# Attention reads, a Fourier mix and an MLP on one core: the first axis of batch 0 copied ahead of the last table sines and the Exp table load

## The chip, the core and the metric

The kernel runs on one core of a Trainium2 chip. The metric is the device time of one execution, in microseconds, as the median of several executions. Inside a profile, times count from the first instruction of the span (325.0 us in the profiled execution).

A core has TensorE (PE: matmuls, and PEld: its weight loads), VectorE (DVE), ScalarE (ACT), GpSimd (POOL) and SyncE (SP, which here only issues transfers). Each engine works through its own instructions in the order of the program and waits where a buffer or an operand is not ready. All engines are scheduled by hand in this kernel: the order of the calls in the source is the order on each engine.

## The reference, cut to what matters

`x` is 8 x 8 x 512 x 64 (batch, head, position, depth), `state` is 8 x 8 x 32 x 64. Positions read from the state, the state reads from the positions, and both go together into a Fourier mix over 544 positions and 512 channels, followed by a normalised two-layer MLP.

```python
def _attn_ref(x, state):
    scores = scale * np.matmul(x, state.transpose(0, 1, 3, 2))
    ...                                     # softmax over the 32 state rows
    xread = np.matmul(a, state)
    scores2 = scale * np.matmul(state, x.transpose(0, 1, 3, 2))
    ...                                     # softmax over the 512 positions
    sread = np.matmul(a2, x)
    return np.concatenate([xread, sread], axis=2)

def _moe_ref(x, w_ch1, w_ch2):              # x: 8 x 544 x 512
    X = np.fft.fft(x, axis=1)
    X = np.fft.fft(X, axis=2)
    u = x + np.real(X)
    ...                                     # mean and variance over the channels
    un = (u - mu) / np.sqrt(var + 1e-06)
    ch = np.maximum(un @ w_ch1, 0.0) @ w_ch2
    return u + ch
```

The real part of the two transforms is computed as matmuls with tables of cosines and sines: first over the positions ("the first axis", tables CT, ST and, for the rows from 256 on, CL and SL), then over the channels (tables TE and TO). The symmetry of the tables is used: inputs are folded first (XE, XO, XQ), so that fewer rows have to be multiplied.

## The kernel before

Batches are worked through as a pipeline. For each batch, `attend` gives the reads, `transform` the Fourier mix U, its mean and its centred and transposed copy, `layer1` and `layer2` the MLP. The opening is special, because the tables have to be made and nothing of a batch before is there to fill TensorE. `warm(n)` are n matmuls of 128 columns whose result nobody reads; they keep TensorE busy in the opening.

The tables, all on ScalarE (the arguments q1, f1, q2_, f2 come from DVE):

```python
    def sines():
        w = 2.0 * PI / Stot * shrink
        nc.scalar.activation(CT, q1[:, 0:2, :], AF.Sin, bias=halfpi, scale=-w)
        nc.scalar.activation(ST, f1[:, 0:2, :], AF.Sin, bias=0.0, scale=w)
        nc.scalar.activation(CL[0:32, 0, :], q1[0:32, 2, :], AF.Sin, bias=halfpi[0:32], scale=-w)
        nc.scalar.activation(SL[0:32, 0, :], f1[0:32, 2, :], AF.Sin, bias=0.0, scale=w)

    def more_sines():
        # ... eight sines of 128 columns: TE and TO (L241 to L248) ...
        w = 2.0 * PI / Stot * shrink
        nc.scalar.activation(cl1, q1[:, 2, :], AF.Sin, bias=halfpi, scale=-w)      # L250
        nc.scalar.activation(sl1, f1[:, 2, :], AF.Sin, bias=0.0, scale=w)          # L251
        nc.scalar.activation(gate2[:, 3:4], gate2[:, 0:1], AF.Exp)                 # L252
```

`cl1` and `sl1` are the low tables: GpSimd copies them into CL and SL for batches 1 to 3 (and 5 to 7). The Exp at the end, of one column, is there to have ScalarE's table for Exp loaded before the scores of batch 1 need it; Sin and Exp have different tables.

`more_loads` holds what GpSimd does next, in order: two sign rows of TO, the cast of x of batch 1 (behind a small copy that waits for the last XQ of batch 0), some clears, the low tables' copies, the load of x of batch 2, the casts of the state, and the load of w2 (behind a small copy that waits for x of batch 2).

x of a batch is transposed on TensorE and copied out of PSUM (batch 0 to 2):

```python
        def turn_x(g):
            # ... b >= 3: by transfers ...
            p = psF.tile([128, 1024], BF16, name="xTp", tag="c") if b == 1 else qt("xTp", BF16)
            for si in (0, 1, 3, 2):
                for k in range(2):
                    o = k * 512 + si * 128
                    nc.tensor.transpose(p[:, o:o + 128], xin[:, si, ...], ident)
            (nc.vector.tensor_copy if b == 0 or g == (b == 1) else nc.scalar.copy)(
                xT[:, 2 * g:2 * g + 2, :], p.rearrange("p (a b) -> p a b", b=S))        # L346
```

`qt` takes a buffer of a PSUM pool with three of them. The first axis, four products `gp`, each copied to one part of G; XQ[:, j] are the folded inputs, made by DVE one after the other:

```python
        def over_s(j):
            p = qt("gp")
            tab = cos if j < 2 else sin
            for c in range(3):
                nc.tensor.matmul(p[:, 0:NM], lhsT=XQ[:, j, c, :], rhs=tab[c], ...)     # L505
            if j == 2:
                for c in range(3):
                    nc.tensor.matmul(p[:, 0:NM], lhsT=XN[:, c, :], rhs=cos[c], ...)    # L509
            if b == 0 and j == 3:
                nc.vector.tensor_copy(G[:, j, :], p[:, 0:NM])                          # L511
            else:
                nc.scalar.copy(G[:, j, :], p[:, 0:NM])                                 # L513
            ...
```

The second axis (`second_axis`, L470 and L471) multiplies all four parts of G with TE and TO into `yp`, in the order of parts 0, 2, 1, 3; U is `yp` plus the read (L475, DVE), then come mean and variance (L302, L304, DVE), the centred copy `ub` (L537, ScalarE, for batches 0 and 1), its transposes on TensorE (L548) and their copy `unT` (L549), which layer 1 reads (L635 for batch 0).

The order of the opening. `t0` are the steps of `transform(0)`: 0 to 3 the four products of the first axis, 4 and 8 the second axis of the two row tiles, 5, 6, 10, 11 U and ub, 7, 9, 12, 13 the transposes of ub. `s1` are batch 1's steps up to its scores (0 its state's transposes, 1 and 2 those of x, 3 to 6 scores), `r1` its reads (0 and 1 the first two, 3 to 5 and 7 the others and the fold), `L` and `M` the two layers of batch 0:

```python
    weave((warmed(r0, 4), 0, 1), ([sines], 0.25, 0.25), ([more_sines], 0.3, 0.3), ([lambda: warm(44)], 1, 1))
    more_loads()
    load_x(3)
    ...
    for step in (warmed(t0[:4], 2) + [
            t0[4], t0[8], W(6), s1[1], W(4), t0[5], s1[0], W(16), t0[7], t0[6], s1[2], L[0], s1[3], t0[9], L[1], t0[10], s1[4],
            L[2], t0[11], t0[12], L[3], s1[5], L[4], s1[6], t0[13], r1[0], L[5], L[6], r1[1],
            L[7], r1[3], L[8], r1[4], L[9], r1[5], L[10], r1[7], late_cast]):
        step()
```

`late_cast` has GpSimd cast x of batch 2. After this list come the rest of layer 1, layer 2 and the pipeline of batches 1 to 7.

Of the kernel before, what the change touches and what calls it, by code (L numbers as in the profile page):

```python
# [28 lines left out]
def kernel(  # L29
# [8 lines left out]
    nc = tc.nc  # L38
# [72 lines left out]
    def load_x(b):  # L111
        xs = wk.tile([128, 4, dm], F32, name="xs", tag="xs")
        xb = x[b].rearrange("h s d -> s h d")
        for n, (ps, si, rows) in enumerate((
            (slice(0, 128), 2, xb[256:384]),
            (slice(0, 128), 0, xb[1:129]),
            (slice(0, 128), 1, xb[129:257]),
            (slice(0, 128), 3, xb[384:512]),
            (slice(0, 1), 2, xb[0:1]),
        )):  # L120
            queue = nc.scalar if b == 0 and n in (1, 3) else nc.sync
            queue.dma_start(out=xs[ps, si, :].rearrange("p (h d) -> p h d", d=D), in_=rows)
        xs_of[b] = xs

    def cast_x(b):
        xs, t = xs_of[b], xin_bufs[b % 2]
        if b == 0:
            for si in (0, 1, 3, 2):
                nc.scalar.copy(t[:, si, 1:513], xs[:, si, :])
        else:  # L130
            nc.gpsimd.tensor_copy(t[:, :, 1:513], xs)  # L131
# [12 lines left out]
    def state_blocks(lo, hi, copy=nc.scalar.copy):  # L144
        for hh in range(4):
            pq = slice(32 * hh, 32 * hh + 32)
            copy(stb[pq, lo:hi, :, 4 + 64 * hh:68 + 64 * hh], stf[pq, lo:hi, :, :])
# [86 lines left out]
    def low_tables(hh):  # L234
        pq = slice(32 * hh, 32 * hh + 32)
        nc.gpsimd.tensor_copy(CL[pq, hh, :], cl1[pq])
        nc.gpsimd.tensor_copy(SL[pq, hh, :], sl1[pq])

    def more_sines():
        w = 2.0 * PI / dm * shrink  # L240
        nc.scalar.activation(TE[:, 0:128], q2_[:, 0:128], AF.Sin, bias=halfpi, scale=-w)  # L241
        nc.scalar.activation(TE[:, 128:256], q2_[:, 0:128], AF.Sin, bias=sg[:, 2:3], scale=sg[:, 3:4])
        nc.scalar.activation(TO[:, 0:128], f2[:, 256:384], AF.Sin, bias=0.0, scale=-w)
        nc.scalar.activation(TO[:, 128:256], f2[:, 256:384], AF.Sin, bias=0.0, scale=sg[:, 3:4])
        nc.scalar.activation(TE[:, 256:384], q2_[:, 128:256], AF.Sin, bias=halfpi, scale=-w)
        nc.scalar.activation(TE[:, 384:512], q2_[:, 128:256], AF.Sin, bias=sg[:, 2:3], scale=sg[:, 3:4])
        nc.scalar.activation(TO[:, 256:384], f2[:, 128:256], AF.Sin, bias=0.0, scale=-w)
        nc.scalar.activation(TO[:, 384:512], f2[:, 128:256], AF.Sin, bias=0.0, scale=sg[:, 3:4])  # L248
        w = 2.0 * PI / Stot * shrink
        nc.scalar.activation(cl1, q1[:, 2, :], AF.Sin, bias=halfpi, scale=-w)  # L250
        nc.scalar.activation(sl1, f1[:, 2, :], AF.Sin, bias=0.0, scale=w)  # L251
        nc.scalar.activation(gate2[:, 3:4], gate2[:, 0:1], AF.Exp)  # L252

    def alternate():
        for lo, v in ((0, 0.5), (256, 1.0)):
            nc.gpsimd.memset(TO[0:1, lo:lo + 256:2], -v)
            nc.gpsimd.memset(TO[0:1, lo + 1:lo + 256:2], v)
# [4 lines left out]
    def clears(i):  # L262
        nc.gpsimd.memset(XFs[i][:, :, 512:514], 0.0)
        nc.gpsimd.memset(XRs[i][:, :, 0:514:513], 0.0)
        nc.gpsimd.memset(XLs[i][:, 512:514], 0.0)
        if i == 0:
            nc.gpsimd.memset(XE[:, 2, :], 0.0)
            nc.gpsimd.memset(XO[:, 2, :], 0.0)
            nc.gpsimd.memset(XO[:, 0:2, 0:257:256], 0.0)
        nc.gpsimd.memset(XNs[i].rearrange("p a b -> p (a b)"), 0.0)  # L270
# [8 lines left out]
    def more_loads():  # L279
        alternate()  # L280
        nc.gpsimd.tensor_copy(gate[:, 0:1], XQs[0][:, 3, 0, 0:1])
        cast_x(1)
        clears(1)
        nc.gpsimd.memset(stb[:, 2:].rearrange("p b g c -> p (b g c)").bitcast(F32), 0.0)
        for hh in range(1, 4):
            low_tables(hh)
        nc.gpsimd.tensor_tensor(gate, xs_of[0][:, :, 0], w1[:, :, 3 * 512], op=ALU.add)
        load_x(2)
        state_blocks(2, B, nc.gpsimd.tensor_copy)
        nc.gpsimd.tensor_copy(gate, xs_of[2][:, :, 0])  # L290
        for q in range(4):
            nc.gpsimd.dma_start(out=w2[:, q * 4:(q + 1) * 4, :], in_=w2v[:, q * 4:(q + 1) * 4, :])

    def qt(name, dt=F32):
        return psQ.tile([128, 512 if dt == F32 else 1024], dt, name=name, tag="q")
# [20 lines left out]
    def attend(b):  # L316
# [7 lines left out]
        xT = wk.tile([128, 4, S], BF16, name="xT", tag="xT")  # L324
# [11 lines left out]
        def turn_x(g):  # L336
            if b >= x_by_dma:
                for si in ((0, 1), (3, 2))[g]:
                    nc.sync.dma_start_transpose(out=xT[:, :, 128 * si:128 * si + 128], in_=xin[:, si, 1:513])
                return  # L340
            p = psF.tile([128, 1024], BF16, name="xTp", tag="c") if b == 1 else qt("xTp", BF16)
            for si in (0, 1, 3, 2):
                for k in range(2):
                    o = k * 512 + si * 128
                    nc.tensor.transpose(p[:, o:o + 128], xin[:, si, 1 + 128 * (2 * g + k):129 + 128 * (2 * g + k)], ident)
            (nc.vector.tensor_copy if b == 0 or g == (b == 1) else nc.scalar.copy)(  # L346
                xT[:, 2 * g:2 * g + 2, :], p.rearrange("p (a b) -> p a b", b=S))


# [86 lines left out]
        def fold():  # L436
# [6 lines left out]
            nc.vector.tensor_add(XQ[:, 3], XO[:, :, 128:0:-1], XO[:, :, 128:256])  # L443

        first = ([] if b >= x_by_dma else [turn_state, lambda: turn_x(0), lambda: turn_x(1)]) + [
            lambda: scores_t(0),
            lambda: scores_t(1),
# [3 lines left out]
        if b >= x_by_dma:  # L451
            turned[b] = lambda: (turn_x(0), turn_x(1))
            first.insert(0, turn_state)
# [245 lines left out]
    def weave(*streams):  # L699
        todo = []  # L700
        for n, (steps, lo, hi) in enumerate(streams):
            for i, s in enumerate(steps):
                if s is not None:
                    todo.append((lo + (hi - lo) * (i + 0.5) / len(steps), n, i, s))
        for _, _, _, s in sorted(todo, key=lambda t: t[:3]):
            s()

    def warm(n):
        t = psF.tile([128, 512], F32, name="warm", tag="c")
        for i in range(n):  # L710
            nc.tensor.matmul(t[:, 0:128], lhsT=ident, rhs=ident, start=(i == 0), stop=(i == n - 1))  # L711

    def warmed(steps, n):
        return [lambda s=s: (s(), warm(n)) for s in steps if s is not None]
# [3 lines left out]
    s1, reads_next = attend(1)  # L718
    t0 = transform(0)
    weave((warmed(s0[:4], 8) + s0[4:], 0, 1), ([lambda: state_blocks(1, 2, nc.vector.tensor_copy)], 0.7, 0.7))  # L720
    weave((warmed(r0, 4), 0, 1), ([sines], 0.25, 0.25), ([more_sines], 0.3, 0.3), ([lambda: warm(44)], 1, 1))
    more_loads()
    load_x(3)
    scores_next, reads_after = attend(2)
    L, M, r1, t1 = layer1(0), layer2(0), reads_next, transform(1)
    W = lambda n: (lambda: warm(n))
# [2 lines left out]
        cast_x(2)  # L729
        state_ones(2, B)  # L730

    for step in (warmed(t0[:4], 2) + [
            t0[4], t0[8], W(6), s1[1], W(4), t0[5], s1[0], W(16), t0[7], t0[6], s1[2], L[0], s1[3], t0[9], L[1], t0[10], s1[4],
            L[2], t0[11], t0[12], L[3], s1[5], L[4], s1[6], t0[13], r1[0], L[5], L[6], r1[1],
            L[7], r1[3], L[8], r1[4], L[9], r1[5], L[10], r1[7], late_cast]):
        step()
    weave((L[11:], 0, 0.27), (t1, 0.2, 0.9), ([M[i] for i in (0, 4, 1, 5, 2, 6, 3, 7)], 0.36, 1),
# [51 lines left out]
```

The softmax here doesn't subtract the row's maximum and nothing guards it: scores larger than these inputs give would overflow.

## Time and profile before

| what | value |
|---|---|
| time, median of three runs | 325.43 us (325.41 to 326.77) |
| span of the profiled execution | 325.0 us |
| mean granted TensorE clock | 0.995 |
| instructions | 5777 |
| share of the chain that ended last | PE 79%, DVE 11%, ACT 6%, issue 2%, POOL 1% |
| transfers | 33.17 MB, mean 102 GB/s |
| table loads on ScalarE | three, 1.28 us each, at 1.92, 17.63 and 24.15 us |

The views used are these. The page gives each engine's busy time, and the span in 40 slices (8.1 us each) with the TensorE clock that was granted, in tenths of full speed. The chain of waits follows the work that ended last back from the end, at each step to what released it; its rows are start, length, engine, tile and line. The timeline lists instructions in order of time: start, length, engine, line, operation, what is written from what is read, and in brackets the idle time ahead of it and what ended that. The view by stretches gives, for each stretch, its length, the busy time and the number of instructions of PE, PEld, DVE, ACT and POOL, then the granted clock (1.00 is full speed), the busy share of the transfer engines, and GB/s.

### The profile page before, as it was taken

The page shows a single profiled execution, that of the slowest core. Times are in us where ns is not written, and L with a number is a line of the kernel's source. Part 1 is how long each engine was busy: PE and PEld are TensorE (multiplying, and loading weights), DVE is VectorE, ACT ScalarE, POOL GpSimd, SP SyncE. Part 2 cuts the span into 40 slices and gives each one's busy share as a digit, 9 for nine tenths or more (in the row PEclk, how much of TensorE's full clock was granted, in tenths as well). Part 3 has the DMA queues.
Part 4 walks back from the last instruction along what each step waited for, and adds up shares of the span by engine and source line. Part 5 has one row for each costly group of instructions (what it writes and reads, how often), then busy time and mean ns, then how long its engine had stood idle before and what let it go on. Part 6 is the DMA issues. An engine that isn't in the chain of part 4 may idle for free.

```text
span 325.0 us, 5777 instructions
## 1 busy us (share of the span) xinstructions
PE 310.1 (95%) x2214; PEld 182.4 (56%) x2214; DVE 190.7 (59%) x456; ACT 145.2 (45%) x281; POOL 73.0 (22%) x165
## 2 busy tenths in 40 slices
PE   5977999999999999999999999999999999999995
PEld 5856987554555555555555554545554544455444
DVE  8794667758677783881825966486737693100112
ACT  6695855654553434333354344433434432344200
POOL 7559933410150021300330015000300030000000
PEclk9997999999999999999999999999999999999999
DMA  7999990606747924268242433630252115302056
GB/s 139 212 198 173 214 174 9 122 34 144 147 74 159 177 48 90 57 143 149 68 97 64 100 67 81 130 83 32 47 118 52 47 32 129 81 34 65 35 118 141
DMA packets 107084, 33.17 MB, mean 102 GB/s; under 512 B 98480, under 2 KB 102832, under 8 KB 107056
## 3 DMA queue, kind: packets, MB, share of 16 engines
q1 hardware_dynamic: 96336, 27.03, 39.7%
q0 software_dynamic: 4224, 4.19, 7.9%
q10 hardware_dynamic: 6496, 1.57, 2.3%
q8 instruction: 17, 0.28, 0.4%
q14 instruction: 11, 0.09, 0.1%
HBM read 22.04 MB, written 13.63 MB: 110 GB/s over the span
## 4 chain that ended last, share of the span: by engine, by line
PE 79%; DVE 11%; ACT 6%; issue 2%; POOL 1%; DVEq 0%; POOLq 0%; ACTq 0%
PE po L691 31%; PE ph L625 29%; PE gp L505 3%; PE warm L711 2%; PE ph L635 2%; PE eTp L354 2%; DVE U L475 2%; PE srp L401 1%; DVE st L302 1%; PE yp L471 1%; PE yp L470 1%; PE po L683 1%; DVE XR L391 1%; PE xrp L382 1%; ACT XR L412 1%
## 5 line engine op out<-in xcount | busy, mean ns | idle before, releaser
L691 PE MATMUL po<-w,hT 128*128 128x512 bf16 x496 | 125.0, 379 | 0.0
L625 PE MATMUL ph<-unT,w 128*128 128x512 bf16 x448 | 114.6, 379 | 0.9 <-DVE ot L656 0.8
L627 ACT ACTIVATE hT<-ph 128x512 bf16<-128x512 f32 x112 | 66.8, 597 | 104.1 <-PE ph L625 104.0
L625 PEld LDWEIGHTS <-w 128*128 128x128 bf16 x576 | 51.0, 98 | 48.2 <-issue 1.7
L691 PEld LDWEIGHTS <-hT 128*128 128x128 bf16 x496 | 47.9, 98 | 45.7
L656 DVE SCALAR_TENSOR_TENSOR ot<-po,rstd,U 128x512 f32<-128x512 f32 (+1 forms) x33 | 24.2, 732 | 58.7 <-PE po L691 51.7
L515 POOL COPY GL<-G 128x128 bf16<-128x128 bf16 x8 | 2.4, 300 | 122.8 <-ACT G L513 122.8
L302 DVE BATCH_NORM_STATS2 st<-U 128x6 f32<-128x512 f32 x32 | 21.8, 682 | 0.1
L306 POOL TENSOR_TENSOR rstd<-mv,epst 128x1 f32<-128x1 f32 x34 | 7.7, 227 | 60.4 <-DVE mv L304 60.4
L307 POOL TENSOR_TENSOR rstd<-rstd,mhalf 128x1 f32<-128x1 f32 x34 | 20.1, 592 | 2.7
L412 ACT ACTIVATE XR<-srp,rcs 32x64 bf16<-32x64 f32 x36 | 11.1, 309 | 20.8 <-DVE rcs L403 20.2
L711 PE MATMUL warm<-ident 128*128 128x128 bf16 x182 | 16.3, 249 | 3.5 <-POOL ident masks.py:199 3.4
L513 ACT CAST G<-gp 128x288 bf16<-128x288 f32 x31 | 12.1, 397 | 12.2 <-PE gp L505 6.2
L711 PEld LDWEIGHTS <-ident 128*128 128x128 bf16 x182 | 14.3, 115 | 4.4 <-POOL ident masks.py:199 3.4
L635 PE MATMUL ph<-unT,w 128*128 128x128 bf16 x256 | 16.2, 219 | 0.2 <-ACT unT L549 0.2
L635 PEld LDWEIGHTS <-w 128*128 128x128 bf16 x256 | 15.1, 98 | 0.6 <-issue 0.3
L475 DVE TENSOR_TENSOR U<-yp,XR 128x512 f32<-128x512 f32 x16 | 10.9, 682 | 6.2 <-PE yp L471 6.2
L505 PEld LDWEIGHTS <-XQ 128*128 128x128 bf16 x96 | 8.8, 98 | 10.3 <-DVE XQ L438 3.4
L131 POOL CAST xin<-xs 128x2048 bf16<-128x2048 f32 x7 | 13.2, 1891 | 0.0
L539 DVE TENSOR_SCALAR ub<-U,mv 128x512 bf16<-128x512 f32 x24 | 12.2, 508 | 1.1 <-DVE mv L304 0.3
L382 PEld LDWEIGHTS <-ET 128*128 128x128 bf16 x80 | 7.2, 98 | 9.2 <-DVE XL L391 0.8
L391 DVE TENSOR_TENSOR XR<-xrp,rs 128x512 bf16<-128x512 f32 x16 | 11.1, 694 | 0.7
(173 smaller groups left out, 375.1 us busy)
## 6 DMA issues: line engine op xcount, KB each, us to landing
xs<-in_x_dram SPq DMA_DIRECT2D x30, 256.0 KB, 4.6
w<-in_moe_w_ch_dram POOLq DMA_DIRECT2D x8, 512.0 KB, 10.3
out_dram<-ot SPq DMA_DIRECT2D x15, 256.0 KB, 2.3
r_dram<-ot SPq DMA_DIRECT2D x14, 256.0 KB, 2.3
out_dram<-r_dram SPq DMA_DIRECT2D x14, 256.0 KB, 3.7
xs<-in_x_dram ACTq DMA_DIRECT2D x2, 256.0 KB
l_dram<-ot SPq DMA_DIRECT2D x2, 256.0 KB, 2.0
r_dram<-ot ACTq DMA_DIRECT2D x2, 256.0 KB
```

The source lines that it names most:

```text
L302: nc.vector.bn_stats(st6, u)
L307: nc.gpsimd.tensor_tensor(rstd, rstd, mhalf, op=ALU.pow)
L391: nc.vector.tensor_tensor(ov, in0=p[ps, :, 0:256].rearrange("p g (h d) -> p g h d", d=D), in1=rs[ps].unsqueeze(3).to_broadcast([n, 2, 4, D ...
L412: nc.scalar.activation(o, i, AF.Copy, scale=rcs[ph, g:g + 1])
L475: nc.vector.tensor_add(u.rearrange("p (k r) -> p k r", r=2), p.rearrange("p (r k) -> p k r", r=2)[:, 0:u.shape[1] // 2, :], x.rearrange("p ...
L505: nc.tensor.matmul(p[:, 0:NM], lhsT=XQ[:, j, c, :], rhs=tab[c], start=(c == 0), stop=(c == 2 and j != 2))
L625: nc.tensor.matmul(ph[:, o:o + n], lhsT=w1[:, c, f * 128:(f + 1) * 128], rhs=un_of[key][:, c, :], start=(c == 0), stop=(c == DC - 1))
L627: nc.scalar.activation(hT[:, per * i:per * i + per, :].rearrange("p a b -> p (a b)"), ph, AF.Relu, scale=-1.0 if key in flipped else 1.0)
L635: nc.tensor.matmul(ph[:, o:o + 128], lhsT=w1[:, c, f * 128:(f + 1) * 128], rhs=un_of[key][:, c, 128 * r:128 * r + 128], start=(c == 0), st ...
L656: nc.vector.scalar_tensor_tensor(ot[:, cols], in0=po_of[i][:, 0:cols.stop - cols.start], scalar=rstd, in1=u[:, cols], op0=ALU.mult, op1=AL ...
L691: nc.tensor.matmul(po_of[i], lhsT=h_of[key][:, f, i * 128:(i + 1) * 128], rhs=w2[:, f, :], start=(f == 0), stop=(f == FC - 1))
L711: nc.tensor.matmul(t[:, 0:128], lhsT=ident, rhs=ident, start=(i == 0), stop=(i == n - 1))
```

## The change

Three things are done in one diff. The two low sines and the Exp are taken out of `more_sines` and placed later, between the products of the first axis: ScalarE now copies the first two parts of G, then makes the low tables, then copies the third part, and only then loads the Exp table. `more_loads` and the load of x of batch 3 move with them, so that the low tables are still made ahead of GpSimd's copies of them. The copies of the transposed x of batch 0 are shared by DVE and ScalarE, half each. And batch 1's first read, `r1[0]`, moves ahead of the fifth step of layer 1. It is meant to have ScalarE hand out the first axis as soon as it is there, and do what is needed later in the time that follows.

```diff
         nc.scalar.activation(TO[:, 384:512], f2[:, 128:256], AF.Sin, bias=0.0, scale=sg[:, 3:4])
+
+    def last_sines():
         w = 2.0 * PI / Stot * shrink
         nc.scalar.activation(cl1, q1[:, 2, :], AF.Sin, bias=halfpi, scale=-w)
         nc.scalar.activation(sl1, f1[:, 2, :], AF.Sin, bias=0.0, scale=w)
+
+    def exp_again():
         nc.scalar.activation(gate2[:, 3:4], gate2[:, 0:1], AF.Exp)
 ...
-            (nc.vector.tensor_copy if b == 0 or g == (b == 1) else nc.scalar.copy)(
+            if b == 0:
+                nc.vector.tensor_copy(xT[:, 2 * g, :], p[:, 0:512])
+                nc.scalar.copy(xT[:, 2 * g + 1, :], p[:, 512:1024])
+                return
+            (nc.vector.tensor_copy if g == (b == 1) else nc.scalar.copy)(
                 xT[:, 2 * g:2 * g + 2, :], p.rearrange("p (a b) -> p a b", b=S))
 ...
-    more_loads()
-    load_x(3)
+    load_x3 = lambda: load_x(3)
 ...
-    for step in (warmed(t0[:4], 2) + [
+    for step in (warmed(t0[:2], 2) + [last_sines, more_loads, load_x3] + warmed(t0[2:4], 2) + [exp_again,
             t0[4], t0[8], W(6), s1[1], W(4), t0[5], s1[0], W(16), t0[7], t0[6], s1[2], L[0], s1[3], t0[9], L[1], t0[10], s1[4],
-            L[2], t0[11], t0[12], L[3], s1[5], L[4], s1[6], t0[13], r1[0], L[5], L[6], r1[1],
+            L[2], t0[11], t0[12], L[3], s1[5], r1[0], L[4], s1[6], t0[13], L[5], L[6], r1[1],
             L[7], r1[3], L[8], r1[4], L[9], r1[5], L[10], r1[7], late_cast]):
         step()
```

## The prediction

> **What bounds the kernel now.** I read the page's engine rows and its 40 slices first, then the chain of waits in order of time for the opening, then the timeline of the engines between 20 and 33 us, and last the busy time and granted clock in stretches of 1 us. From the page:
>
> ```profile
> PE 310.1 (95%) x2214; PEld 182.4 (56%) x2214; DVE 190.7 (59%) x456; ACT 145.2 (45%) x281; POOL 73.0 (22%) x165
> PEclk9997999999999999999999999999999999999999
> ```
>
> TensorE is busy for 95% of the span. The table by stretches has it busy for 99.4 of the 100 us from 100 to 200, and 99.7 of those from 200 to 300. Nothing on another engine can shorten that; what can be won is TensorE's idle time in the opening, and the fourth slice (24.4 to 32.5 us), where its clock is below full. The chain of waits there (start, length, engine, tile, line):
>
> ```profile
> 23.38 0.42 ACT gen L250
> 23.80 0.33 ACT gen L251
> 24.15 1.28 ACT L252
> 25.45 0.20 ACT gate L252
> 25.65 0.02 issue
> 25.67 0.41 ACT G L513
> 26.08 0.04 issue
> 26.12 0.84 PE gp L505 x3
> ...
> 30.11 1.01 ACT xT L346
> 31.12 0.62 ACT ub L537
> 31.74 0.48 ACT sT L334
> 32.23 0.59 ACT unT L549
> 32.83 0.04 issue
> 32.87 1.05 PE ph L635 x16
> ```
>
> ScalarE holds the path from 15.05 to 26.08 us without a gap: the reads of batch 0, the sines, the two sines of the low tables (L250, L251), the table load for Exp (L252), and only then the copies of the first axis, G (L513). The timeline shows what stood ready while they queued:
>
> ```profile
> 22.23 0.29 PE L505 MATMUL gp<-CL,XQ 128*128 128x288 bf16 x1
> 26.12 0.60 PE L505 MATMUL gp<-ST,XQ 128*128 128x288 bf16 x2 [1.33 <-ACT G L513]
> 25.67 1.00 ACT L513 CAST G<-gp 128x288 bf16<-128x288 f32 x3
> 23.64 0.55 DVE L443 TENSOR_TENSOR XQ<-XO 128x384 bf16<-128x384 f32 x1
> 27.00 0.46 DVE L511 CAST G<-gp 128x288 bf16<-128x288 f32 x1 [2.81 <-PE gp L505]
> ```
>
> The first product gp was complete at 22.52 us and was not copied before 25.67. The PSUM pool has three buffers, so the fourth product waited 1.33 us for a buffer, though its XQ had been ready at 24.19. The clock in the stretches behind it:
>
> ```profile
> 25.00:26.00 1.00, 0.00 (x0) 0.00 (x0) 0.00 (x0) 0.96 (x4) 1.00 (x1) 1.00 0.88 146
> 27.00:28.00 1.00, 1.00 (x7) 0.66 (x6) 0.45 (x1) 0.00 (x0) 1.00 (x1) 0.50 0.19 45
> ```
>
> TensorE does nothing from 25 to 26, and runs at half clock after that: 0.60 between 26 and 27, 0.50 until 29.5, 0.89 in the half after. That is about 3.4 us, in which a matmul of 256 columns took 0.21 us from start to start where those of batch 1 (57 to 58 us) took 0.11.
>
> [...] The trace shows ScalarE's copies and casts without a load of their own, with three loads in all, but always under the Exp set; under the sine set no run here shows it yet. [...]
>
> **The change, part by part.**
>
> *1. G ahead of the low tables' sines and the load.* On ScalarE two copies move in front of L250, and a third in front of the load. From the last table sine (L248, 22.99 + 0.39) on, starts follow one another by 0.30 us for copies (three in 1.00 us, 0.40 each), and by 0.42 and 0.33 for the two sines:
> - G0 at 23.28 to 23.68, instead of 25.67; G1 23.58 to 23.98;
> - L250 at 23.88, L251 at 24.30, free at 24.63 to 24.73;
> - gp2 is complete at 24.69 (24.40 + 0.29, unchanged, since it waits for DVE's XQ), so G2 runs 24.72 to 25.12;
> - the load from 25.14 to 26.42, Exp until 26.64, beside TensorE, while ScalarE has nothing else to do.
>
> On TensorE the fourth product no longer waits: its buffer is free at 23.68 and its XQ ready at 24.19, so it follows gp2 and two warm-up matmuls at 24.64, not 26.12. At full clock three matmuls take 0.37 and the tail 0.16, so it is there at 25.18; DVE's G3 (0.46) is ready at 25.68; the fourth yp matmul of the first row tile starts at 25.72 and ends at 25.99. U is then added at 26.03 instead of 28.14, **2.1 us earlier**.
>
> The path after it goes through batch 1's transposes, which stand on TensorE in front of U's own. Four more yp matmuls (0.44) and six warm-ups (0.33) put them at 26.60, not 29.32. Their input, GpSimd's cast of x (24.44 + 1.90 = 26.34), is just in time. They end at 27.2, so ScalarE's xT copy (L346) runs from 27.23, not 30.11. The ub (U's mean is ready at 26.03 + 0.69 + 0.03 + 0.69 + 0.04 + 0.18 = 27.66, so ScalarE is last), the sT copy and unT follow at the old distances, 32.87 - 30.11 = 2.76 later: the first matmul of layer 1 at 29.99, not 32.87. **Gain 2.88 us**: 1.48 in the fourth product's start, the rest because TensorE stays at full clock between there and the transposes (26.12 to 29.32 is 3.20 us; 24.64 to 26.60 is 1.96, with the new 0.37 us wait for G3 in it).
>
> *2. x of batch 0 copied by two engines.* DVE's two copies of 128x1024 (0.69 each) become copies of 128x512 on both: 0.42 on DVE (as L549's) and 0.57 on ScalarE (as L334's). ScalarE is free for the first at 10.16 (after sT) and for the second at 11.02, so the copies end at 10.74 and 11.60, instead of 10.82 and 11.71. But the scores that read them start at 11.27 and 12.15, behind warm-up matmuls: in the chain of waits TensorE goes from 3.42 to 12.76 without a wait. **Gain 0.**
>
> *3. Batch 1's first read before the fifth layer-1 step.* TensorE issues without a gap from 32.87 to 42; the move alters the order of the same matmuls. DVE gets XR an estimated 1.3 us sooner (one step of 0.89, a score of 0.23 and a transpose of 0.22), then waits for the second read as before. **Gain 0 to 0.2**; I count 0.
>
> *4. The loads move in program order* between the second and the third product, with GpSimd's queue in the same order. Its next work still waits for XQ at 24.19, so nothing moves there.
>
> From 32.87 on all engines follow TensorE, so the lead should travel to the end. What stays at fixed times is the transfers. w1: the DMA share falls from 1.25 to 0.17 at 26 us, so it is in. w2, first read at 53.90, is issued from 34.50 by a GpSimd chain that doesn't move; the DMA share falls to 0.05 at 48 us, and the first read would be at 51.0: 3 us of room. The sum is 325.43 - 2.88 = 322.55, and I say **322.6 us**.
>
> **The rivals.**
>
> *A copy among sines costs a table load.* Then one or two more loads of 1.28 us stand before G, and G2 comes after 26 us; some 1.3 to 2.6 us are lost and the time is 324 to 325.5. The three loads in all speak against it. I give it 5%.
>
> *The clock drops all the same, or elsewhere.* TensorE still has idle gaps of 1.01 us before 21.98 and 0.67 before 23.77. If half clock falls on the transposes, 0.4 to 0.7 us are lost (323.0 to 323.3). If it falls on the dense layer-1 stretch, 3.4 us at half rate lose up to 1.7 (324.3). [...] 20%.
>
> *Another wait takes the gain.* GpSimd's cast holds the transposes at 26.34, so a part done sooner wins nothing; w2 could be late; the table load, now beside TensorE's work, could meet the xT copy: it has 0.6 us of room (26.64 to 27.23). These would leave 323 to 324. 15%.
>
> *It gains more.* If batch 1's chain on DVE is shortened by the early read, TensorE's later waits (0.45 us for GpSimd's xin at 55.38, 0.71 for ub at 65.50) shrink: 322.0.
>
> **Range and chances.** The bulk lies at 322.2 to 323.2; the clock and the late waits stretch it upwards to 324.4, the gain in the later waits and the scatter of a run downwards to 321.6. Faster by over 2% would need 318.9 us, that is 6.5 us, more than all of TensorE's idle time between 20 and 33 us (3.6 us) and the half clock's loss together: 0.02. Slower by over 2% would need a wait of 6.5 us in the path that no part of the diff makes: 0.01. Within 2%: 0.97.
>
> **What would show each step.** In the changed profile the third table load begins near 25.1 instead of 24.15, with three casts of G ahead of it and two of them ahead of the low sines; still three loads. The fourth gp starts near 24.6 without waiting for G. The clock reads 1.00 from 26 to 30. U's first add is near 26.0 and layer 1 starts near 30.0. The xT copies of batch 0 appear on two engines, with scores still at 11.3. Later TensorE events (w2's first matmul at 53.90 before) come 2.9 us sooner. A fourth table load, a stretch at 0.50 elsewhere, or a wait for w2 would make the prediction wrong.

## The result and the profile after

The changed kernel takes 323.73 us, the median of four runs (323.58 to 324.05). The kernel before, measured beside it, took 325.99 us (four runs, 325.41, 325.43, 326.54 and 326.77). The ratio is 0.993, with a 95% interval of 0.9903 to 0.9958: faster, by less than 2%. The predicted time was 322.6 us with a range of 321.6 to 324.4. The span of the profiled execution is 322.0 us instead of 325.0.

ScalarE's timeline, at the place where the queue of sines stood:

```profile
22.88 0.38 ACT L248 ACTIVATE TO<-gen,sg 128x128 bf16<-128x128 f32 x1
23.28 0.70 ACT L521 CAST G<-gp 128x288 bf16<-128x288 f32 x2
23.87 0.55 ACT L252 ACTIVATE gen<-gen,halfpi 128x288 bf16<-128x288 f32 x1
24.30 0.44 ACT L253 ACTIVATE gen<-gen 128x288 bf16<-128x288 f32 x1
24.64 0.40 ACT L521 CAST G<-gp 128x288 bf16<-128x288 f32 x1
25.05 1.28 ACT L256 ACT_TABLE_LOAD   x1
```

Two copies of G (L521) stand ahead of the low sines (L252, L253), the third ahead of the load (1.28 us), and no load of its own stands in front of a copy or of the sine behind it. The chain of waits no longer goes through ScalarE's sines:

```profile
23.05 0.57 DVE XQ L450
23.62 0.05 issue
23.66 0.54 PE gp L513 x3
24.21 0.37 PE gp L517 x3
24.57 0.11 PE warm L719 x2
24.68 0.38 PE gp L513 x3
25.07 0.02 issue
25.09 0.47 DVE G L519
...
26.66 0.46 PE xTp L349 x8
27.12 0.02 issue
27.14 1.01 ACT xT L354
28.16 0.62 ACT ub L545
28.78 0.47 ACT sT L338
29.25 0.01 issue
29.27 0.59 ACT unT L557
29.86 0.04 issue
29.90 1.05 PE ph L643 x16
```

VectorE's XQ now sets the first axis; the fourth product follows the third; layer 1 starts at 29.90 us, not 32.87. The same stretches as before, with their clock:

```profile
25.00:26.00 1.00, 0.89 (x10) 0.53 (x8) 0.46 (x2) 0.98 (x2) 1.00 (x1) 1.00 0.58 95
27.00:28.00 1.00, 1.00 (x21) 1.00 (x19) 0.96 (x3) 0.85 (x1) 1.00 (x1) 1.00 0.33 78
```

TensorE is at work from 25 to 26 us, and its clock stays at 1.00. The span is 3.0 us shorter, almost the 2.88 that was predicted, and yet the median time fell by 2.26, and against the median that the prediction started from (325.43) by only 1.70. The profiled execution of before took 326.84 us by its own time, and that of the changed kernel 323.83. That gap between one execution and the median is what the experiments had to explain.

### The profile page after: what moved, and what is told of

Its sections match the earlier page's. It is cut to its first block, busy times and chain, and to the rows that moved or that the text cites. A ratio compares the mean times of both kernels' runs of the same rounds, so it can differ in the third digit from the quotient of the medians.

```text
span 322.0 us, 5748 instructions
## 1 busy us (share of the span) xinstructions
PE 305.8 (95%) x2183; PEld 179.9 (56%) x2214; DVE 190.5 (59%) x456; ACT 146.2 (45%) x283; POOL 72.1 (22%) x165
## 4 chain that ended last, share of the span: by engine, by line
PE 78%; DVE 13%; ACT 3%; issue 2%; DMA 2%; POOL 1%; SPq 0%; DVEq 0%; ACTq 0%; POOLq 0%
PE po L699 31%; PE ph L633 29%; PE gp L513 3%; PE ph L643 2%; DMA xs<-in_x_dram 2%; PE eTp L362 2%; PE srp L409 2%; DVE U L483 2%; DVE st L306 1%; PE yp L479 1%; DVE XR L399 1%; PE po L691 1%; PE xrp L390 1%; PE yp L478 1%; PE esp L373 1%
## 5 line engine op out<-in xcount | busy, mean ns | idle before, releaser
L699 PE MATMUL po<-w,hT 128*128 128x512 bf16 x477 | 122.8, 379 | 0.8
L310 POOL TENSOR_TENSOR rstd<-mv,epst 128x1 f32<-128x1 f32 x34 | 6.5, 191 | 61.5 <-DVE mv L308 61.5
L719 PE MATMUL warm<-ident 128*128 128x128 bf16 x182 | 14.5, 232 | 3.5 <-POOL ident masks.py:199 3.4
L521 ACT CAST G<-gp 128x288 bf16<-128x288 f32 x31 | 12.1, 396 | 12.2 <-PE gp L513 6.2
L719 PEld LDWEIGHTS <-ident 128*128 128x128 bf16 x182 | 12.7, 104 | 4.2 <-POOL ident masks.py:199 3.4
```

Source lines behind the costliest of these rows:

```text
L699: nc.tensor.matmul(po_of[i], lhsT=h_of[key][:, f, i * 128:(i + 1) * 128], rhs=w2[:, f, :], start=(f == 0), stop=(f == FC - 1))
```

## The experiments

A useful yardstick came out of the traces: the time from the first product of the first axis to the start of layer 1, and to batch 2's first product. It leaves out how late the first product starts (between 21.7 and 22.1 us in these executions) and when the last store ends. All numbers are differences of start times in the timelines of TensorE; the clock is the mean granted one of the profiled execution.

| kernel | first product at | to layer 1 | to batch 2's first product | clock |
|---|---|---|---|---|
| before | 21.98 | 10.89 | 57.48 | 0.995 |
| before, again | 22.13 | 10.87 | 57.46 | 0.995 |
| only the split copies | 21.71 | 9.56 | 56.14 | 0.999 |
| only the early read | 21.68 | 9.64 | 56.23 | 0.998 |
| before with fill | 21.70 | 9.56 | 56.15 | 1.000 |
| changed | 21.86 | 8.04 | 54.63 | 1.000 |
| only the order | 21.97 | 8.04 | 54.64 | 1.000 |
| only the load behind G | 21.73 | 8.07 | 54.67 | 0.998 |
| load ahead of G2 | 21.78 | 9.25 | 55.84 | 1.000 |
| two PSUM tiles | 22.12 | 8.77 | 55.36 | 1.000 |
| transposes later | 21.97 | 7.71 | 54.47 | 0.999 |
| transposes and scores later | 21.84 | 7.71 | 54.44 | 0.999 |

**1. Only the order on ScalarE.** The changed kernel, with the copies of batch 0's x and the first read as before:

```diff
-            if b == 0:
-                nc.vector.tensor_copy(xT[:, 2 * g, :], p[:, 0:512])
-                nc.scalar.copy(xT[:, 2 * g + 1, :], p[:, 512:1024])
-                return
-            (nc.vector.tensor_copy if g == (b == 1) else nc.scalar.copy)(
+            (nc.vector.tensor_copy if b == 0 or g == (b == 1) else nc.scalar.copy)(
...
-            L[2], t0[11], t0[12], L[3], s1[5], r1[0], L[4], s1[6], t0[13], L[5], ...
+            L[2], t0[11], t0[12], L[3], s1[5], L[4], s1[6], t0[13], r1[0], L[5], ...
```

> Only the order on ScalarE changes (G0 and G1 ahead of the two low sines, G2 ahead of the Exp load); x of batch 0 is copied by VectorE alone and batch 1's first read stays where it was. Theory (the order is the whole gain): span 322.0 to 322.2 us, as the changed kernel, layer 1 from 29.9 to 30.0 us. Rival (the two other parts carry some of the gain): 322.6 us or more.

Measured: 324.01 us (ratio to before 0.9954, interval 0.994 to 0.9968), span 322.4, 8.04 us to layer 1 and 54.64 to batch 2, the changed kernel's to a hundredth. Layer 1 starts at 30.01. The span is 0.2 us over what the theory allowed. Against the changed kernel's 322.0, 0.11 us stand ahead of the first product (21.97 instead of 21.86) and the rest behind batch 2's. It is below the rival's 322.6. The medians are 0.28 us apart and the runs overlap (323.75 to 324.39 here). Up to batch 2 the order is the whole gain.

**2. Only the split copies**, in the kernel before (the first hunk above, the other way round).

> Only the copies of the transposed x of batch 0 are shared by VectorE and ScalarE, in the kernel before. Theory (the copies stand behind warm-up matmuls): 325.0 us of span within 0.2, scores at 11.2 to 11.3 us; ScalarE's half starts only after VectorE's, as the changed kernel's trace shows, and the pair ends near 11.05 and 11.95 us instead of 10.82 and 11.71. Rival (a free VectorE brings batch 0's reads forward): 324.5 us or less.

Measured: 325.23 us, ratio 0.9996 (0.9981 to 1.0011): no difference. But the profiled execution had a span of 323.4 and a clock of 0.999, and reached layer 1 in 9.56 us instead of 10.89. By itself that would have spoken for the rival. But the first product follows the first score by 10.71 us (11.00 to 21.71), exactly as in the kernel before (11.27 to 21.98), so the split won nothing between these two; the difference arises later, in the stretch with the half clock.

**3. Only the early read**, in the kernel before (the second hunk above, the other way round).

> Only batch 1's first read is moved ahead of the fifth step of layer 1, in the kernel before. Theory (same matmuls in another order, VectorE then waits for the second read as before): 325.0 us of span within 0.2. Rival (the early read shortens batch 1's chain of reads): 324.4 us or less, with the cast of x of batch 2 before 53.3 us.

Measured: 325.26 us, ratio 0.9996 (0.9981 to 1.0011): no difference. Again the profiled execution had 323.4 us and no half clock, although this edit touches nothing before the fifth step of layer 1. So the edit can't be what lifted the clock, and the profile of before was not that of every execution.

**4. More warm-up matmuls where TensorE stood idle**, in the kernel before:

```diff
-    for step in (warmed(t0[:4], 2) + [
+    for step in (warmed(t0[:3], 2) + [W(20)] + warmed(t0[3:4], 2) + [
```

> The kernel before with 20 more warm-up matmuls behind the third product of the first axis, so that TensorE is busy while it waits for ScalarE; the order on ScalarE is that of before. Theory (a good part of the gain is the clock): clock 1.00 from 26 to 30 us, fourth product still at 26.1 us, batch 1's transposes near 28.1 instead of 29.3 us, layer 1 near 31.4, span 323.5 us, a gain of 1.4. Rival (the half clock lies beside the path, the wait is all): span 325.0 within 0.2.

Measured: 325.27 us (ratio 0.9993, 0.9982 to 1.0004), span 323.4. The trace is as the theory had it: the fourth product at 25.88, batch 1's transposes at 27.86, layer 1 at 31.26. But its median is that of before. Both fit once the runs are sorted by their mean clock. The kernel before ran 87 times beside these experiments:

| mean granted clock | runs | time, median | time, range | span, range |
|---|---|---|---|---|
| 0.998 to 1.000 | 64 | 325.31 | 325.16 to 325.72 | 323.4 to 323.9 |
| 0.995 | 23 | 326.86 | 326.53 to 327.49 | 324.8 to 325.7 |

No run lies between. The half clock falls on about a quarter of the executions, which take 1.55 us longer (326.86 - 325.31); the profile of before showed one of them. The fill removed it, in 14 of 14 runs, and left the typical run where it was.

**5. Only the Exp load behind the copies of G**; the low sines ahead of them all, as before:

```diff
-    for step in (warmed(t0[:2], 2) + [last_sines, more_loads, load_x3] + warmed(t0[2:4], 2) + [exp_again,
+    for step in ([last_sines] + warmed(t0[:2], 2) + [more_loads, load_x3] + warmed(t0[2:4], 2) + [exp_again,
```

> The changed kernel with the two low sines again ahead of all copies of G; only the Exp load stays behind the copies. Theory (the load is what had to move: G2 can't start before its product is there at 24.6 us, and G0 is needed only by then): G0 from 24.0, G1 from 24.3, G2 from 24.7, fourth product at 24.6 us, span 322.0 within 0.1. Rival (the two sines ahead of G count too): 322.6 us or more.

Measured: 323.91 us (ratio 0.9937, 0.9915 to 0.9958), span 321.9, 8.07 us to layer 1. The changed kernel's time, without moving the sines. ScalarE's timeline of this run:

```profile
23.10 0.52 ACT L252 ACTIVATE gen<-gen,halfpi 128x288 bf16<-128x288 f32 x1
23.52 0.43 ACT L253 ACTIVATE gen<-gen 128x288 bf16<-128x288 f32 x1
23.97 1.00 ACT L521 CAST G<-gp 128x288 bf16<-128x288 f32 x3
24.99 1.28 ACT L256 ACT_TABLE_LOAD   x1
```

G0 comes 0.7 us later than in the changed kernel and is still early enough: the last copy can't start before its product, at 24.6 us, and the fourth product needs its buffer no sooner.

**6. The load ahead of the third copy**; the first two copies stay ahead of the sines:

```diff
-    for step in (warmed(t0[:2], 2) + [last_sines, more_loads, load_x3] + warmed(t0[2:4], 2) + [exp_again,
+    for step in (warmed(t0[:2], 2) + [last_sines, exp_again, more_loads, load_x3] + warmed(t0[2:4], 2) + [
```

> The changed kernel with the Exp load placed straight behind the two low sines, ahead of the third copy of G; the first two copies stay ahead of the sines. Theory: fourth product still at 24.6 us, but G2 at 26.2 instead of 24.6, so the second axis is finished 1.2 us later than in the changed kernel: span 323.2 us if the clock stays full, up to 324.4 if TensorE's idle 1.3 us halves it again. Rival (freeing PSUM buffers early is what counts): 322.0 within 0.2.

Measured: 325.05 us (ratio 0.9974, 0.9962 to 0.9986), span 323.2, 9.25 us to layer 1: 1.21 over the changed kernel, as expected, with the clock at full in all 22 runs. TensorE's timeline:

```profile
24.92 0.27 PE L478 MATMUL yp<-TE,G 128*128 128x256 bf16 x1
26.52 0.28 PE L479 MATMUL yp<-TO,G 128*128 128x256 bf16 x1 [1.33 <-ACT G L521]
```

The PSUM buffers were free and the fourth product done, and the wait of 1.33 us has only moved from the fourth product to the second matmul behind it. With experiment 5: the load's place behind the third copy makes most of the gain, 1.21 us. While the load stays ahead of it, the early copies of G0 and G1 are still worth 0.31 us (9.25 us to layer 1 instead of the 9.56 of experiments 2 and 4): the fourth product comes 2.66 us after the first here, and 4.18 in experiment 2. Once the load is behind G2, they are worth nothing.

**7. Two PSUM tiles for the two copies of batch 0's x**, in the changed kernel:

```diff
             if b == 0:
+                q = psF.tile([128, 1024], BF16, name="xTq", tag="c")
+                # ... the transposes of k == 1 go to q ...
                 nc.vector.tensor_copy(xT[:, 2 * g, :], p[:, 0:512])
-                nc.scalar.copy(xT[:, 2 * g + 1, :], p[:, 512:1024])
+                nc.scalar.copy(xT[:, 2 * g + 1, :], q[:, 0:512])
```

> The changed kernel with the two halves of the transposed x of batch 0 in two PSUM tiles instead of one. Theory (the two engines' copies wait for one another because they read one tile): both copies start within 0.1 us of one another, ScalarE's ends near 10.6 and 11.5 instead of 11.05 and 11.96 us; the scores stay at 11.1 and 12.0, so the span is 322.0 within 0.2. Rival (ScalarE is held by something else): its copy still starts 0.4 us after VectorE's.

In the changed kernel ScalarE's half waits for VectorE's:

```profile
10.02 0.42 DVE L351 COPY xT<-xTp 128x512 bf16<-128x512 bf16 x1 [0.30 <-PE xTp L349]
10.47 0.58 ACT L352 COPY xT<-xTp 128x512 bf16<-128x512 bf16 x1 [0.36 <-DVE xT L351]
```

With two tiles it doesn't:

```profile
10.22 0.42 DVE L352 COPY xT<-xTp 128x512 bf16<-128x512 bf16 x1 [0.51 <-PE xTp L350]
10.28 0.58 ACT L353 COPY xT<-xTq 128x512 bf16<-128x512 bf16 x1
```

So the shared tile is what holds it: ScalarE's half starts 0.45 us after VectorE's with one tile, 0.06 us with two. The time is 323.86 us (ratio 0.994, 0.9917 to 0.9964), the changed kernel's. The profiled execution took longer (324.79 us, 323.0 of span and 8.77 us to layer 1), for another reason: GpSimd's cast of batch 1's x waited 0.93 us for the transfer and started at 25.52, not 24.33 as in the changed kernel.

**8. Batch 1's transposes behind the first ub**, in the changed kernel:

```diff
-            t0[4], t0[8], W(6), s1[1], W(4), t0[5], s1[0], W(16), t0[7], t0[6], s1[2], L[0], s1[3], ...
+            t0[4], t0[8], W(10), t0[5], s1[0], W(24), t0[7], s1[1], t0[6], s1[2], L[0], s1[3], ...
```

> The changed kernel with batch 1's first x transposes and their ScalarE copy (1.0 us) moved behind the first transposes of ub, and the warm-up matmuls there raised from 26 to 34. Theory (in the changed kernel the first ub waits 0.4 us for that copy, its mean having been ready at 27.63): ub at 27.65 instead of 28.05, layer 1 near 29.5 instead of 29.9, span 321.6 us. Rival (the copy then delays the second ub and batch 1's scores as much): 322.0 or more.

Measured: 323.69 us (ratio 0.9929, 0.9908 to 0.995), span 322.0. Layer 1 comes 0.33 us sooner (7.71 instead of 8.04), batch 2's first product only 0.16 (54.47). The copy now stands in front of the second ub (which starts 8.40 us after the first product instead of 7.89), and half of the gain is given back: between theory and rival, with no difference in time that these runs can show.

**9. Less fill, in the kernel before**, to see what the half clock hangs on:

```diff
-    for step in (warmed(t0[:4], 2) + [
+    for step in (t0[:4] + [
```

> The kernel before without the four pairs of warm-up matmuls in the first axis. Theory (the clock is halved where TensorE was busy too little over some 3.4 us, and the phase of that window is free, so that only some executions meet it): TensorE's emptiest 3.4 us go from 1.42 us busy to about 1.2, so more executions than the quarter of before take 326.5 us or more; the median is 326.5 to 327. Rival (chance of the single execution, not TensorE's idle time): as before, about a quarter of them, median 325.3.

Measured: median 326.61 us (ratio 1.0013, 0.9996 to 1.003). Eight of 14 runs are at 326.57 us or more, all with a clock of 0.988 to 0.995; the other six lie at 325.19 to 325.65. Without eight matmuls, none of them on the path, the half clock fell on 8 of 14 runs, instead of 23 of 87 (5 of the 25 beside them); with so few runs the ratio is rough.

**10. Less fill, in the changed kernel** (the same edit on its list).

> The changed kernel without the four pairs of warm-up matmuls in the first axis. Theory: its emptiest 3.4 us (from 20.8 us) go from 1.73 us busy to about 1.4, what the kernel before has, so that some executions now meet the half clock and take 1 to 1.5 us more (325 us), most stay at 323.7. Rival (the changed order is safe by itself, whatever the fill): none above 324.4, as in the changed kernel.

Measured: median 323.90 us (ratio 0.9954, 0.9938 to 0.9971). Four of 12 runs have a clock of 0.995 and take 324.80 to 325.16 us; the other eight have a median of 323.76. The new order is not safe by itself; its fill keeps the clock up. The emptiest 3.41 us of its profile hold 1.60 us of matmuls, not the 1.4 expected. In the 34 runs of the changed kernel and of experiments 1, 5, 7, 8 and 11, which all have the fill and the late load, none fell below 0.998.

**11. Batch 1's first scores later as well:**

```diff
-            t0[4], t0[8], W(6), s1[1], W(4), t0[5], s1[0], W(16), t0[7], t0[6], s1[2], L[0], s1[3], t0[9], L[1], t0[10], s1[4],
+            t0[4], t0[8], W(10), t0[5], s1[0], W(24), t0[7], t0[6], s1[1], s1[2], L[0], t0[9], L[1], s1[3], t0[10], s1[4],
```

> The changed kernel with batch 1's x transposes behind the transposes of the first ub, their ScalarE copy behind the second ub, and its first scores behind the second step of layer 1. Theory (the run with only the transposes moved won 0.33 us up to layer 1 and gave 0.17 back to the second ub): nothing is given back; from the first product of the first axis to layer 1 7.7 us instead of 8.04, and to batch 2's first gp 54.3 instead of 54.63; time 323.4 us. Rival (the later scores delay batch 1's reads): 54.6 or more, 323.7.

Measured: 323.65 us (323.55 to 323.84; ratio 0.9931, 0.9911 to 0.9951), span 321.8, 7.71 us to layer 1, 54.44 to batch 2: the second ub now starts at 29.36 us, yet only 0.19 of 0.33 us remains. Where the rest went stays open. The lowest median of all, but six runs do not set it apart from the changed kernel's 323.73.

**12. The kernel before, once more.**

> The kernel before, unchanged, once more with a profile. Theory (the profile shown was of an execution with the half clock, three in four are without): clock 1.00 throughout, 9.6 us from the first product to layer 1 instead of 10.89, span 323.4 us. Rival (the half clock belongs to every execution, and the changes of the experiments removed it): 10.9 us, 325.0.

Measured: 326.93 us, span 325.1, clock 0.995, 10.87 us to layer 1. This single execution met the half clock again, against what I expected, and by itself decides nothing. The 87 runs of experiment 4's table decide: the rival's "every execution" is wrong, for 64 of them kept the clock.

## Why the prediction was right, and where it was not

**The order on ScalarE.** Its steps held one by one. G0 at 23.28 (predicted 23.28), G2 at 24.64 (24.72), the load at 25.05 (25.14), the fourth product at 24.52 (24.64), U's first add at 26.00 (26.03), batch 1's transposes at 26.50 (26.60), layer 1 at 29.90 (29.99). From the first product to layer 1 the profiles went from 10.89 to 8.04 us: 2.85, against 2.88 predicted. But the working made G0 and the freed buffer its hinge. Experiments 5 and 6 put it elsewhere: the load's place behind G2 carries the gain, and with it there the sines' place is worth nothing.

**The term that was mis-sized.** The sum was "325.43 - 2.88 = 322.55". The 2.88 has two parts: 1.48 us for the fourth product's start, and 1.40 for "the rest because TensorE stays at full clock" (1.24 of it ahead of batch 1's transposes, 0.16 in them). The second part is the one that fails. It was read from an execution with the half clock, which took 326.84 us itself, and was subtracted from a median of other executions, most of which never lose the clock. Within one execution it is right: 326.84 - 2.88 = 323.96, and the changed kernel's profiled execution took 323.83. Without the half clock the order of before needs 9.56 us to layer 1 (experiments 2 and 4; 9.64 in experiment 3), not 10.89, so the change saves 9.56 - 8.04 = 1.52 us. From the full-clock median of 325.31 that gives 323.79, and 323.73 was measured. The half clock's share, 1.33 us in that stretch, is saved only in the quarter of executions that had it. Of the four runs of before beside the result two took 326.54 and 326.77 us, as those with the half clock do; so the medians there differ by 2.26 us and not by 1.58 (325.31 - 323.73). The warning stood beside the profile: a clock of 0.995, and a time 1.41 us above the median.

**The range.** 323.73 us lies above the bulk that was given (322.2 to 323.2). The range reaches that far for a clock that drops in the changed kernel and for late waits, and the changed kernel's profile shows neither. That the range holds the result is luck in that part: the room was made for other reasons.

**The rival "the clock drops all the same, or elsewhere"** looked at the wrong kernel. I asked whether the changed kernel might still lose its clock, not whether the kernel before always does. The half clock began at 26.20, 26.50 and 26.43 us in the three profiles that have it, and 64 of 87 runs of before kept the clock: it belongs to some executions, not to every one. I had one profile of before, whose granted clock shows both ends of the half clock, at 26.20 and 29.61 us, and took it for the base. That the clock stays full in the new order was my estimate: it read 0.998 to 1.000 in the four runs of the changed kernel, and 0.995 in 4 of 12 runs of the same order with less fill (experiment 10).

**Copies by two engines.** Gain 0 is right (experiment 2), the working is wrong. I let ScalarE's copy run beside VectorE's and end at 10.74 and 11.60 us. It starts 0.45 us after VectorE's and ends at 11.05 and 11.96, later than VectorE's single copy did before. The trace shows ScalarE idle for 0.36 us until VectorE's copy out of the same tile ends, and experiment 7 that this wait goes with two tiles (starts 0.06 us apart). Why the second copy waits is not shown. The scores still start behind their warm-up matmuls, at 11.15 and 12.04, now with 0.1 us to spare.

**The early read, the loads.** The early read is worth 0, as predicted (experiments 1 and 3), and the rival "it gains more" did not come: TensorE's later waits are still 0.45 us (for xin, at 52.41) and 0.71 (for ub, at 62.53). No run moves the loads alone; experiment 6, which moves them, loses most of the gain, so they don't carry it. GpSimd's cast of batch 1's x stayed where it was (24.33 us, 24.44 before). But "just in time" left out the transfer of that x: in experiment 7's profile it arrives as late as 25.5 us, and layer 1 then comes 0.73 us later (8.77 instead of 8.04).

**A copy among sines costs a load.** Refuted. There are three loads as before, of 1.28 us each, at 1.92, 17.52 and 25.05 us. Between the second and the third, copies of G stand before the low sines (from 23.28 us) and after them (at 24.64): under the sine set too, the changed kernel's trace shows copies without a load of their own.

**Travel to the end.** From layer 1 to batch 2's first product it is 46.59 us before (57.48 - 10.89) and changed (54.63 - 8.04) alike. The lead neither grew nor shrank; w2 was in time.

## What to carry to other kernels

When ScalarE must switch tables, put the switch behind the last copy that somebody waits for (here a load of 1.28 us, whose place was worth 1.21); the order of the copies and sines in front of it was worth nothing here, as long as none was late. A gain read from one profile is a gain of that execution: compare its clock and its time with those of the other runs before subtracting it from their median. Splitting a copy between two engines took two PSUM tiles here before the halves ran side by side (starts 0.06 us apart, not 0.45), and it gains nothing while the reader stands behind other work.

## What the runs showed of the hardware that was not expected

Small amounts of work changed how often TensorE's clock halved: without eight warm-up matmuls it did so in 8 of 14 runs of before instead of 23 of 87. In the three profiles with the half clock it lasts from 26.20 to 29.61 us (before), from 26.50 to 29.91 (experiment 12) and from 26.43 to 29.84 (experiment 9), 3.41 us each time. In the 3.41 us just ahead of it, matmuls were busy for 1.42, 1.43 and 1.19 us. The record of before has the clock full for 17.067 us up to 26.20, half for 3.413, and full again for 296.960 up to 326.57: 5, 1 and 87 steps of 3.413 us. That of the changed kernel has it full for 317.440 us from 6.09 on, 93 such steps. A fixed grid of 3.413 us within an execution, on which alone the clock changes, is my estimate from these four lengths; what follows counts with it.

Experiments 2 and 3 leave everything from the first axis to layer 1 as it was before, and kept the clock in their profiles. There it falls only after the last matmul, at 322.57 and 322.26 us. Counted back from there in steps of 3.413 us, stretches of the grid end at 25.61 and 25.30, and they hold 1.67 and 1.95 us of matmuls. Both traces have an emptier 3.41 us, with 1.39 and 1.31, but a border of the grid cuts it in two. The stretch ahead of the drop in before, and that of experiment 2:

```profile
22.78:26.20 3.42, 1.42 (x13) 0.96 (x12) 1.30 (x3) 3.37 (x9) 2.33 (x4) 1.00 1.09 183
22.20:25.61 3.41, 1.67 (x16) 1.15 (x14) 1.62 (x4) 3.36 (x9) 2.22 (x6) 1.00 1.13 189
```

Over all fourteen profiles the emptiest stretch of the grid, from the first full clock to the last matmul of the program, holds 1.19 to 1.43 us in the three that lost the clock and 1.67 to 2.40 in the eleven that kept it. From this an estimate can be made: if a stretch with less than about 1.65 us halves the clock, and the grid starts anywhere with equal chance, the share of executions that meet one is 25% for before, 55% for experiment 9, 20% for experiment 10, 8% for experiment 6, and 0 for the changed kernel and for experiment 4. Counted were 23 of 87 (26%), 8 of 14 (57%), 4 of 12 (33%), none of 22, none of 4 and none of 14. The 1.65 was chosen within the gap so that it fits; at 1.50 the estimates for experiments 9 and 10 would be 26% and 0. No run tests it by itself, and whether busy time is what counts stays open.

In the three profiles with the half clock the first product also started 0.3 to 0.4 us later than in experiments 2 to 4 (22.0 to 22.1 us against 21.7). It follows batch 0's first score by 10.71 us in all six, so the difference arises ahead of that score. There the warm-up matmuls follow one another by 0.107 us until 9.1 to 9.4 us in the three and until about 8.5, 8.2 and 6.6 in experiments 2 to 4, and by 0.056 afterwards: 9.13 us in before is five steps of 3.413 us ahead of the drop at 26.20. The late full clock is the likely cause, but no run changes it alone.
